# All packs from the fifth on turn their exponentials on VectorE and through DRAM; visits placed anew

## The chip, the cores and the metric

One core of one Trainium2 chip runs the whole program. The metric is the device time of that core in microseconds; a time given for a kernel is the median of its runs.

## The reference

Windowed attention of 8 heads (four with a plain window of 32, four with a window of 128 in steps of 4), followed by a gated feed-forward layer:

```python
def _attn_ref(q, k, v):                      # 8 x 8 x 576 x 64
    scores = scale * np.matmul(q, k.transpose(0, 1, 3, 2))
...
    masks = np.stack([mask_plain if h < H // 2 else mask_dil for h in range(H)], axis=0)
    scores = np.where(masks[None, :, :, :], scores, -1000000000.0)
    scores = scores - np.max(scores, axis=-1, keepdims=True)
    attn = np.exp(scores)
    attn = attn / (np.sum(attn, axis=-1, keepdims=True) + 1e-09)
    return np.matmul(attn, v)
...
def _moe_ref(x, w_gate, w_val, w_out):       # 4608 x 512, 512 x 1536, 1536 x 512
    g = x @ w_gate
    silu = g * (1.0 / (1.0 + np.exp(-g)))
    val = x @ w_val
    return (silu * val @ w_out)
```

## The kernel before, in words

**The feed-forward part** is most of the work. Every fp32 number is split into a high and a low part, and a product takes three matmuls (high by high, high by low, low by high). The 4608 tokens go in nine chunks of 512. The first three ("plain") chunks are computed as written: 39 `Item`s, each one block of 128 hidden columns (chunk 0 begins with six items of half width, 256 tokens). An item issues 12 matmuls for the gate into bank `bg` (`gv_mm(it, 0)`), 12 for the value into `bv` (`gv_mm(it, 1)`) and 12 into the four output banks `bo` (`out_mm`), the last ones an item late. Between them ScalarE takes the tanh of `bg` (`act_tanh`), VectorE multiplies twice (`dve_u`, `dve_h`), ScalarE writes the high part (`h_hi`) and GpSimd or VectorE the low part (`h_lo`). A product bank is written again two groups of 12 matmuls after it was filled. The other six chunks are computed by a Strassen scheme with products of 512 columns; it needs sums of weights, which VectorE and ScalarE prepare during the plain chunks (`mix_stage`) and the SyncE queue writes to the DRAM tensor `pieces`.

**The weights** come in 64-bit floating point. 24 units are loaded by SyncE (`w_load`, `at_int<-w`), turned into fp32 by ScalarE and VectorE, and split by ScalarE and by GpSimd (`at_float32r<-at_int`), all within chunk 0. Loading slots are few, so the load of a unit waits until VectorE is done with an earlier one.

**The attention part** comes in 38 packs of 128 x 504 scores, numbered `m` from 0: four packs for each of the first eight chunks, six for the last. Packs 0 to 3 give chunk 0, packs 4 to 7 chunk 1, packs 8 to 11 chunk 2. A pack is worked on in "visits", which the tables of numbers `EARLY`, `LATER` and `SLOTS` (L65 to L73) put at slots between the items: a slot is a third of an item (a group of 12 matmuls) up to slot 116, and one product after it. Chunk 1 begins at slot 45, chunk 2 at slot 81, the Strassen scheme at `SB` = 117. Visit `m` has three parts with a slot for each (`attend`, L886):

- part A: TensorE computes the attention output of an earlier pack `r` (`results`) and the scores of pack `m` (`scores`) into the PSUM tile `two`; VectorE masks, takes the maximum and subtracts it (`shift`), divides the output of pack `r` by its sums (`norm`) and turns it (`turn_y`); ScalarE takes the exponential (`exps`); SyncE loads the next pack's `qkb` and the pack's `vb`.
- part B: the exponentials of pack `m` are transposed, so that the next `results` can use them as weights.
- part C: the finished output of pack `r` is written into the chunk's input, high part by ScalarE, low part by GpSimd or VectorE (`x_copies`).

For part B there are two ways. Up to pack 11 (`m < TURNED`, L63) TensorE transposes four 128 x 128 blocks into PSUM (`turn_e`, L600) and ScalarE copies them to SBUF (`keys`, L604); then `r = m - 1`. From pack 12 on VectorE transposes blocks of 32 x 32 (`turn_far`, L617), SyncE stores the 256 KB to the DRAM tile `turned`, and four DMAs that ScalarE issues read it back in the order wanted (`load_far`, L625, in part A of visit `m + 1`); then `r = m - 2`, and visit `TURNED + 1` has no `results`.

From pack 4 on there is one SBUF buffer of each kind (L522): exponentials `e`, transposed `pt`, values `v`, output `y`. `turn_far` writes its transpose into the buffer `y`, which `norm`, `turn_y` and `x_copies` of pack `r` use too, so `norm` of the next visit waits until the store has read it.

**The order of the work** is written by `Desk`. The program text gives TensorE's order; each other engine's instructions are recorded with costs (L229) and put into an order of their own by a list scheduler (`issue`, L259), DMAs on SyncE and ScalarE among them. Every engine then runs its own list strictly in order. All these instructions appear with line L257 in the profile, those ahead of the recording with L238.

Of the kernel before, what the change touches and what calls it, by code (L numbers as in the profile page):

```python
# [25 lines left out]
NF = DFF // P  # L26
# [33 lines left out]
NSTART = 2  # L60
HALVED = 3
WARM = 9
TURNED = 12  # L63
FREE = 16000, 19500, 17500, 18000, 6000
EARLY = (-1, 1, None), (2, 3.5, 3), (5, 8, 6)  # L65
BEFORE = 3
# [2 lines left out]
ON_ACT = (2, 3, 4, 5, 6, 9, 11, 12, 15, 17, 19, 21, 23)  # L69
START = ("q0 q1 w v0 v1 w Q0 Q1 S0 X0 T0 W0 I3 I2 S1 K0 X1 W1 A0 W2 T1 J2 K1 W3 J2 N0 w U0 q2 v2 A1 q3 w w r W4 H0 W0 "  # L70
         "L0 N1 U1 H1 L1 W1 v3 W2 W3 W4")
LATER = (14, 3, 2), (23, 3, 4), (29, 7, 4), (39, 3, 2)
SLOTS = (1, 4, 7, 10, 13, 17, 20, 23, 27), (4, 13, 25, 37, 48, 58, 72, 84), (2, 11, 20, 29, 39, 47, 54, 65, 74, 84)  # L73
T0 = NPLAIN * CH
NB = S * 8 // CH - 1

# [258 lines left out]
def attention_moe(ctx, tc, qkb, vb, w, const, out):  # L335
# [276 lines left out]
    def at_n(m, n):  # L612

        g, j = divmod(n, NH)
        return n if m < TURNED else NG * j + g

# [205 lines left out]
    def idle(n, bank=k_bank[1]):  # L822
# [12 lines left out]
    first = {  # L835
        "Q": lambda m: scores(m, s_banks[m], True), "S": lambda m: shift(m, s_banks[m], fa, True),
        "X": exps, "T": lambda m: turn_e(m, k_bank[m]), "K": lambda m: keys(m, k_bank[m], fa),
        "A": lambda m: results(m, bank_r), "N": lambda m: norm(m, bank_r, fa),
        "U": turn_y, "H": lambda m: x_copy(m, "hi"), "L": lambda m: x_copy(m, "lo"),
        "q": lambda m: load_qk(m, fa, nc.sync, 2),  # L840
        "v": lambda m: load_v(m, fa, nc.sync, 2),
        "w": lambda m: w_load(3), "r": lambda m: ready.update(w=True), "I": lambda n: idle(n), "J": lambda n: idle(n, k_bank[0]), "W": lambda n: w_one(STAGES[n]),
    }
# [13 lines left out]
    SB = 3 * len(items)  # L857
# [3 lines left out]
    def visits(m, a, b, c):  # L861
        for what, n in zip("ABC", (a, b, c)):
            visit.setdefault(n, []).append((what, m))
# [2 lines left out]
        visits(2 + m, *x)  # L866
    for m, (a, b, c) in enumerate(LATER):
        visits(5 + m, a, a + b, a + c)
    for n in range(4):
        a = SB - 6 * NF + 3 + 25 * n // 3  # L870
        visits(9 + n, a, a + 4, a + 2)
    for n, a in enumerate(SLOTS[0]):
        visits(13 + n, SB - 3 * NF + a, SB - 3 * NF + a + 2, SB - 3 * NF + a + 1)
    first = 22
    for c in range(2):
        for a in SLOTS[1 + c]:
            a += SB + NSLOT * c
            visits(first, a, a + 6, a + 3)
            first += 1

    def ended(m):

        r = m - 1 if m <= TURNED else m - 2
        return r if r >= NSTART and m != TURNED + 1 else None

# [293 lines left out]
    for ci in range(NC):  # L1179
        base = SB + NSLOT * ci  # L1180
        first = n_out(ci, 0, 0)
# [18 lines left out]
        for t in range(NT):  # L1200
            for i in range(NP):
                n = n_out(ci, t, i)
# [59 lines left out]
```

## Time and profile before

| | |
|---|---|
| time, median of 3 runs | 906.27 us (906.18 to 907.73) |
| the profiled execution's own time | 907.4 us |
| its span, first to last instruction | 905.3 us |
| mean granted TensorE clock | 0.998 |
| TensorE matmuls busy | 893.0 us (99% of the span) |
| VectorE / ScalarE / GpSimd busy | 663.0 / 377.7 / 260.8 us (73 / 42 / 29%) |
| DMA | 218.44 MB, mean 241 GB/s |

The span is what the trace covers; the execution's own time is 2.1 us more. The profiled execution lies 1.1 us above the median of the runs.

### The profile page before, as it was taken

What the parts mean: (1) busy time and instruction counts of PE and PEld (TensorE: products, weight loads), DVE (VectorE), ACT (ScalarE), POOL (GpSimd) and SP (SyncE); (2) the same over time, 40 slices, a digit from 0 to 9 for tenths busy, and PEclk for the clock granted to TensorE, in tenths of its full rate; (3) what the DMA queues carried; (4) which work ended last, traced back from release to release, by engine and by line L of the source; (5) the groups of instructions that cost most, each with busy time, mean ns of one, the idle gap of its engine ahead of it and who ended that gap; (6) DMA issues with size and microseconds to landing.
All of it is one profiled execution on the core that took longest, in us unless ns stands there. A gap on an engine that the chain in (4) does not pass through costs nothing.

```text
span 905.3 us, 20915 instructions
## 1 busy us (share of the span) xinstructions
PE 893.0 (99%) x8610; PEld 732.9 (81%) x8610; DVE 663.0 (73%) x1001; ACT 377.7 (42%) x585; POOL 260.8 (29%) x177
## 2 busy tenths in 40 slices
PE   7899999999999999999999999999999999999998
PEld 5887888888878888888888888888888888888886
DVE  6888689888688564877779977878697746556752
ACT  5887433333233233333345543433355433334452
POOL 2569612221311111101132720111146401213451
PEclk9999999999999999999999999999999999999999
DMA  9999986444388751888787678889866675655562
GB/s 348 363 336 347 367 286 237 156 178 148 129 273 271 253 196 37 296 283 266 263 276 262 219 256 283 309 276 308 263 216 214 219 241 190 198 194 189 194 221 93
DMA packets 96142, 218.44 MB, mean 241 GB/s; under 512 B 9904, under 2 KB 37168, under 8 KB 96048
## 3 DMA queue, kind: packets, MB, share of 16 engines
q1 hardware_dynamic: 80928, 210.19, 67.9%
q10 hardware_dynamic: 15120, 6.92, 3.0%
q8 instruction: 68, 1.11, 0.5%
q14 instruction: 26, 0.21, 0.1%
HBM read 167.79 MB, written 49.28 MB: 240 GB/s over the span
## 4 chain that ended last, share of the span: by engine, by line
PE 89%; DMA 7%; DVE 1%; ACT 1%; issue 1%; POOL 0%; SPq 0%; ACTq 0%; DVEq 0%; POOLq 0%
PE bo L257 42%; PE bg L257 21%; PE bv L257 21%; PE two L257 5%; DMA at_int<-w 3%; DMA at_float<-turned 2%; DMA at_float<-qkb 1%; DVE at_int L257 1%; DMA at_float<-vb 1%; DVE at_float L257 0%; POOL at_float32r L257 0%; ACT at_int L257 0%; ACT at_float32r L257 0%; SPq L238 0%; ACTq L257 0%
## 5 line engine op out<-in xcount | busy, mean ns | idle before, releaser
L257 PE MATMUL bo<-at_float32r 128*128 128x512 f32 x1296 | 306.9, 391 | 0.0
L257 PEld LDWEIGHTS bo<-at_float32r 128*128 128x128 f32 x1296 | 242.4, 188 | 51.1
L257 POOL TENSOR_TENSOR at_float32r<-at_float,at_float32r 128x512 fp32r<-128x512 f32 (+1 forms) x109 | 161.2, 1483 | 376.1 <-ACT at_float32r L257 213.7
L257 ACT CAST at_float32r<-at_float 128x512 fp32r<-128x512 f32 (+2 forms) x214 | 147.7, 705 | 157.7 <-DVE at_float L257 76.9
L257 DVE TENSOR_TENSOR at_float<-bo,at_float 128x512 f32<-128x512 f32 x168 | 114.5, 686 | 99.7 <-ACT at_float L257 65.1
L257 DVE TENSOR_TENSOR at_float32r<-at_float,at_float32r 128x512 fp32r<-128x512 f32 (+1 forms) x105 | 114.2, 1103 | 49.2 <-ACT at_float32r L257 37.7
L257 PE MATMUL bg<-at_float32r 128*128 128x512 f32 x486 | 128.2, 390 | 0.0
L257 PE MATMUL bv<-at_float32r 128*128 128x512 f32 x486 | 128.0, 390 | 0.0
L257 ACT ACTIVATE at_float<-at_float 128x512 f32<-128x512 f32 (+1 forms) x108 | 68.0, 631 | 132.7 <-DVE at_float L257 112.1
L257 POOL TENSOR_TENSOR at_float<-at_float,at_float 128x512 f32<-128x512 f32 x36 | 51.0, 1416 | 223.4 <-DVE at_float L257 222.4
L257 PE MATMUL bg<-at_float32r,at_float32r 128*128 128x512 f32 (+1 forms) x468 | 108.6, 380 | 1.6 <-POOL at_float32r L238 0.9
L257 PEld LDWEIGHTS bv<-at_float32r 128*128 128x128 f32 x486 | 91.1, 188 | 19.0
L257 PEld LDWEIGHTS bg<-at_float32r 128*128 128x128 f32 x486 | 91.0, 188 | 19.1
L257 PE MATMUL bv<-at_float32r,at_float32r 128*128 128x512 f32 (+1 forms) x468 | 106.4, 377 | 0.0
L257 PE MATMUL bo<-at_float32r,at_float32r 128*128 128x512 f32 (+1 forms) x468 | 106.3, 376 | 0.0
L257 DVE SCALAR_TENSOR_TENSOR at_float<-at_float,at_float 128x512 f32<-128x512 f32 x144 | 104.8, 730 | 1.0
L257 PEld LDWEIGHTS bg<-at_float32r,at_float32r 128*128 128x128 f32 x468 | 83.4, 190 | 18.8 <-POOL at_float32r L238 1.3
L257 PEld LDWEIGHTS bv<-at_float32r,at_float32r 128*128 128x128 f32 x468 | 83.2, 189 | 16.4 <-DVE at_float L257 0.6
L257 PEld LDWEIGHTS bo<-at_float32r,at_float32r 128*128 128x128 f32 x468 | 82.9, 188 | 16.2
L257 ACT COPY at_float<-bg 128x512 f32<-128x512 f32 x63 | 36.9, 586 | 86.5 <-PE bg L257 78.2
L257 DVE TENSOR_TENSOR at_float<-at_float,at_float 128x512 f32<-128x512 f32 (+2 forms) x80 | 69.0, 873 | 1.6 <-POOL at_float L257 1.2
L257 ACT COPY at_float<-bv 128x512 f32<-128x512 f32 x63 | 37.0, 587 | 34.3 <-PE bv L257 29.7
(74 smaller groups left out, 610.8 us busy)
## 6 DMA issues: line engine op xcount, KB each, us to landing
at_float32r<-pieces SPq DMA_DIRECT2D x189, 512.0 KB, 4.0
pieces<-at_float32r SPq DMA_DIRECT2D x126, 256.0 KB, 4.4
at_float<-qkb SPq DMA_DIRECT2D x32, 576.0 KB, 7.3
at_float<-vb SPq DMA_DIRECT2D x34, 520.0 KB, 5.8
at_int<-w SPq DMA_DIRECT2D x38, 384.0 KB, 6.4
out<-at_float SPq DMA_DIRECT2D x36, 256.0 KB, 4.1
turned<-at_float SPq DMA_DIRECT2D x26, 256.0 KB, 4.0
at_float<-turned ACTq DMA_DIRECT2D x104, 64.0 KB, 6.8
```

The lines of the kernel that those rows point to most:

```text
L257: self.kept.append([engine, lambda: f(*a, **k), sorted(m for m in after if m >= 0), cost, later, both, start])
```

## The change

`TURNED` goes from 12 to 4: packs 4 to 11 take the way of `turn_far` and `load_far` as well. The visit without `results` is now visit 5 and no longer visit 13, and from visit 6 on a visit finishes pack `m - 2`. The slots are set anew so that each chunk's packs are finished where they were: chunk 0 gets five visits after the early ones (slots 14, 23, 28, 33, 39, part B three slots behind A and part C two) where it had four (14, 23, 29, 39); chunk 1 has four (49, 58, 66, 73) where it had four; chunk 2 has eight (83 to 108) where it had nine (82 to 108). The visits in the Strassen part keep their number and shift by up to two slots. The functions that are called are all there before.

```diff
--- before.py
+++ after.py
@@ -60,7 +60,7 @@
 NSTART = 2
 HALVED = 3
 WARM = 9
-TURNED = 12
+TURNED = 4
 FREE = 16000, 19500, 17500, 18000, 6000
 EARLY = (-1, 1, None), (2, 3.5, 3), (5, 8, 6)
 BEFORE = 3
@@ -69,8 +69,8 @@
 ON_ACT = (2, 3, 4, 5, 6, 9, 11, 12, 15, 17, 19, 21, 23)
 START = ("q0 q1 w v0 v1 w Q0 Q1 S0 X0 T0 W0 I3 I2 S1 K0 X1 W1 A0 W2 T1 J2 K1 W3 J2 N0 w U0 q2 v2 A1 q3 w w r W4 H0 W0 "
          "L0 N1 U1 H1 L1 W1 v3 W2 W3 W4")
-LATER = (14, 3, 2), (23, 3, 4), (29, 7, 4), (39, 3, 2)
-SLOTS = (1, 4, 7, 10, 13, 17, 20, 23, 27), (4, 13, 25, 37, 48, 58, 72, 84), (2, 11, 20, 29, 39, 47, 54, 65, 74, 84)
+LATER = (14, 3, 2), (23, 3, 2), (28, 3, 2), (33, 3, 2), (39, 3, 2)
+SLOTS = (4, 13, 21, 28), (2, 5, 8, 12, 16, 19, 23, 27), (2, 13, 23, 37, 48, 58, 72, 84), (4, 11, 19, 29, 37, 47, 54, 65, 74, 84)
 T0 = NPLAIN * CH
 NB = S * 8 // CH - 1
 
@@ -866,14 +866,14 @@
         visits(2 + m, *x)
     for m, (a, b, c) in enumerate(LATER):
         visits(5 + m, a, a + b, a + c)
-    for n in range(4):
-        a = SB - 6 * NF + 3 + 25 * n // 3
-        visits(9 + n, a, a + 4, a + 2)
-    for n, a in enumerate(SLOTS[0]):
-        visits(13 + n, SB - 3 * NF + a, SB - 3 * NF + a + 2, SB - 3 * NF + a + 1)
-    first = 22
+    first = 5 + len(LATER)
     for c in range(2):
-        for a in SLOTS[1 + c]:
+        for a in SLOTS[c]:
+            a += SB - 3 * NF * (2 - c)
+            visits(first, a, a + 4 - 2 * c, a + 2 - c)
+            first += 1
+    for c in range(2):
+        for a in SLOTS[2 + c]:
             a += SB + NSLOT * c
             visits(first, a, a + 6, a + 3)
             first += 1
```

How this moves instructions is shown at three places.

TensorE, chunk 0, the second half of the half-width items (`at_192_bfloat_61` is the identity, `at_512_float_124` the exponentials, `at_1024_float32r` the chunk's input), where part B of pack 4 stood; one piece of the difference:

```order
 L257 MATMUL bo_394<-at_512_float32r,at_1536_float32r 128x256
 L257 MATMUL bv<-at_1024_float32r,at_1536_float32r 128x256 x12
-L257 MATMUL two<-at_192_bfloat_61,at_512_float_124 128x128 x4
 L257 MATMUL bg<-at_1024_float32r,at_1536_float32r 128x256 x12
 L257 MATMUL bv<-at_1024_float32r,at_1536_float32r 128x256 x12
```

The four transposes are gone and nothing takes their place; the same holds for packs 5 to 11, eight times four instructions in all.

VectorE, part A of a visit in chunk 0 (`two` is the PSUM tile, `at_512_float_289` the buffer `y`, `at_512_float_124` the exponentials, `444` and `445` the two buffers of `dve_u` and `dve_h`). Before, visit 7 at slot 29:

```order
L257 TENSOR_TENSOR at_512_float_124<-two,at_384_bfloat_60 128x2x4x63
L257 TENSOR_SCALAR at_8_float_288<-two 128x8
L257 TENSOR_REDUCE at_8_float_238<-at_512_float_124 128x8
L257 RECIPROCAL at_8_float_288<-at_8_float_288 128x8
L257 TENSOR_TENSOR at_512_float_289<-two,at_8_float_288 128x8x2x32
L257 STREAM_TRANSPOSE at_512_float_289<-at_512_float_289 128x512
L257 SCALAR_TENSOR_TENSOR at_512_float_444<-at_512_float_444,bg 128x512
L257 TENSOR_TENSOR at_512_float_124<-at_512_float_124,at_8_float_238 128x2x4x63
```

Now, visit 8 at slot 33:

```order
L257 SCALAR_TENSOR_TENSOR at_512_float_444<-at_512_float_444,bv 128x512
L257 STREAM_TRANSPOSE at_512_float_289<-at_512_float_124 128x512
L257 SCALAR_TENSOR_TENSOR at_512_float_445<-at_512_float_445,bg 128x512
L257 TENSOR_SCALAR at_8_float_288<-two 128x8
L257 TENSOR_TENSOR at_512_float_124<-two,at_384_bfloat_60 128x2x4x63
L257 RECIPROCAL at_8_float_288<-at_8_float_288 128x8
L257 TENSOR_REDUCE at_8_float_227<-at_512_float_124 128x8
L257 TENSOR_TENSOR at_512_float_124<-at_512_float_124,at_8_float_227 128x2x4x63
L257 TENSOR_TENSOR at_512_float_289<-two,at_8_float_288 128x8x2x32
L257 SCALAR_TENSOR_TENSOR at_512_float_445<-at_512_float_445,bv 128x512
L257 STREAM_TRANSPOSE at_512_float_289<-at_512_float_289 128x512
```

The second row is `turn_far` of pack 7, which fills `y`; seven rows on, `norm` writes `y` again, and `dve_h` of the item stands behind it. Before, nothing but VectorE, ScalarE and GpSimd had to do with `y` here.

ScalarE, chunk 0, where the transposed exponentials of pack 6 come into the buffer `pt` (`at_512_float_241`; `turned_58` is a DRAM tile). Before:

```order
L257 ACTIVATE at_512_float_124<-at_512_float_124 128x8x63
L257 CAST at_512_float32r<-at_512_float_444 128x512
L257 CAST at_1536_float32r<-at_776_int_450 128x768
L257 CAST at_1536_float32r<-at_776_int_244 128x768
L257 COPY at_512_float_241<-two 128x512
L257 ACTIVATE at_1536_int_155<-at_1536_int_155 128x768
```

Now:

```order
L257 CAST at_512_float32r<-at_512_float_445 128x512
L257 ACTIVATE at_1536_int_155<-at_1536_int_155 128x768
L257 DMA at_512_float_241<-turned_58 32x4x128 x4
L257 ACTIVATE at_512_float_444<-bg 128x512
L257 CAST at_1024_float32r<-at_512_float_289 128x2x256
L257 ACTIVATE at_512_float_124<-at_512_float_124 128x8x63
L257 CAST at_1536_float32r<-at_1536_int_145 128x768
```

The copy from PSUM is gone. In its place four DMA issues stand directly ahead of an item's tanh (`at_512_float_444<-bg`), and they wait for the store of the same tile to land.

## Rows read from the trace of the kernel before

**Rows 1.** The page's part 1, busy time and instructions of each engine

```profile
PE 893.0 (99%) x8610; PEld 732.9 (81%) x8610; DVE 663.0 (73%) x1001; ACT 377.7 (42%) x585; POOL 260.8 (29%) x177
```

**Rows 2.** Waits of TensorE: who for whom, us in total, times, longest

```profile
PE two L257 <- DMA at_float<-qkb: 2.0, 3, 1.3
PE two L257 <- DMA at_float<-turned: 1.0, 2, 0.7
```

**Rows 3.** Timeline of TensorE, chunk 0: start, length, instructions [idle before]

```profile
107.56 2.88 PE L257 MATMUL bg<-at_float32r,at_float32r 128*128 128x512 f32 x12
110.29 0.60 PE L257 MATMUL two<-at_bfloat,at_float 128*128 128x128 f32 x4
110.64 3.00 PE L257 MATMUL bv<-at_float32r,at_float32r 128*128 128x512 f32 x12
113.48 2.89 PE L257 MATMUL bo<-at_float32r,at_float32r 128*128 128x512 f32 x12
```

**Rows 4.** Timeline of TensorE at the transposes of packs 4 and 5

```profile
40.46 0.74 PE L257 MATMUL bg<-at_float32r,at_float32r 128*128 128x256 f32 x4 [0.24 <-DVE at_float32r L257]
...
77.85 2.88 PE L257 MATMUL bo<-at_float32r,at_float32r 128*128 128x512 f32 x12
80.90 0.66 PE L257 MATMUL two<-at_bfloat,at_float 128*128 128x128 f32 x4 [0.17 <-ACT at_float L257]
```

**Rows 5.** Groups by shape: count, busy us, mean ns of one, idle before

```profile
L257 PE MATMUL two<-at_bfloat,at_float 128*128 128x128 f32 x36 | 5.5, 274 | 0.3 <-ACT at_float L257 0.2 <-DVE at_float L257 0.2
L257 ACT COPY at_float<-two 128x512 f32<-128x512 f32 x9 | 5.2, 580 | 1.6 <-PE two L257 1.6
L257 DVE STREAM_TRANSPOSE at_float<-at_float 128x512 f32<-128x512 f32 x62 | 43.8, 706 | 4.4 <-ACT at_float L257 3.4
L257 DVE TENSOR_TENSOR at_float<-two,at_float 128x512 f32<-128x512 f32 x36 | 24.7, 685 | 0.4
L257 DVE SCALAR_TENSOR_TENSOR at_float<-at_float,bv 128x512 f32<-128x512 f32 x33 | 22.6, 683 | 13.0 <-PE bv L257 12.5
```

**Rows 6.** The tile `turned`: issues (ns min/median/max), and landing times

```profile
L257 ACTq DMA_DIRECT2D at_float<-turned x104: 309/392/2067, 232.0 to 660.8; - x104
...
DMA to landing us min/median/max: 1.9/6.0/9.9
```

**Rows 7.** Three stretches of chunk 0: busy time by engine, clock, DMA share, GB/s

```profile
60.00:80.00 20.00, 19.97 (x215) 16.30 (x214) 19.24 (x21) 15.18 (x21) 16.19 (x9) 1.00 0.97 326
80.00:100.00 20.00, 19.83 (x211) 16.06 (x210) 17.81 (x20) 12.59 (x18) 17.30 (x10) 1.00 1.05 359
100.00:120.00 20.00, 20.00 (x180) 16.38 (x181) 12.81 (x22) 7.78 (x11) 8.12 (x5) 1.00 1.04 364
```

**Rows 8.** Timeline, GpSimd's weight splits and TensorE, chunk 0

```profile
50.65 4.18 POOL L257 TENSOR_TENSOR at_float32r<-at_int,at_float32r 128x768 fp32r<-128x768 f32 x2
...
62.23 2.91 PE L257 MATMUL bg<-at_float32r,at_float32r 128*128 128x512 f32 x12
...
70.82 0.80 PE L257 MATMUL two<-at_float,at_float 64*32 64x65 f32 x60
...
72.24 3.06 PE L257 MATMUL bg<-at_float32r,at_float32r 128*128 128x512 f32 x12
```

**Rows 9.** Timeline, ScalarE's queue and TensorE in chunk 2

```profile
257.06 1.98 ACTq L257 DMA_DIRECT2D at_float<-turned  x4
...
265.89 0.30 PE L257 MATMUL two<-at_float,at_float 64*32 64x65 f32 x2
266.93 0.78 PE L257 MATMUL two<-at_float,at_float 64*32 64x65 f32 x58 [0.74 <-DMA at_float<-turned]
```

**Rows 10.** DMA issues from 60 to 100 us: size, median us to landing

```profile
pieces<-at_float32r SPq DMA_DIRECT2D x23, 256.0 KB, 6.8
at_float<-qkb SPq DMA_DIRECT2D x2, 576.0 KB, 7.9
```

**Rows 11.** Waits of SyncE's queue: us in total, times, longest

```profile
SPq L257 <- DVE at_float32r L257: 74.7, 13, 11.0
```

## The prediction

> **What bounds the kernel now.** I began with the busy shares: TensorE has matmuls in flight for 893.0 of the 905.3 us [rows 1], so only a shorter list for TensorE, or a wait of TensorE that goes or comes, can move the time. Next I read TensorE's waits. The transfers of `qkb` and `turned`, the two that this change can touch, cost it 2.0 and 1.0 us in the whole span [rows 2]. In the three stretches of chunk 0 on which the change bears most, TensorE is busy for 19.97, 19.83 and 20.00 of 20 us [rows 7]. Then I went to the timeline to see what one set of transposes costs TensorE, and last to VectorE, the DMA engines and the queues, to see whether chunk 0 has room for what is added: VectorE is busy for 19.24, 17.81 and 12.81 of 20 us there, and the DMA share is 0.97 to 1.05 [rows 7]. So TensorE sets the pace, and close behind it in chunk 0 stand VectorE and the DMA.
>
> **What goes: 32 transposes on TensorE.** In the timeline I measure from start to start, since the ends of pipelined matmuls are modelled. A group of 12 starts at 107.56, and what follows it at 110.29: 2.73 us. The four transposes of a pack start there and the next group at 110.64: 0.35 us. That group takes 2.84 us to the start of the one after it, 113.48, which is 0.11 us over 2.73 [rows 3]. One pack costs 0.46 us. The mean of a single transpose, 274 ns [rows 5], would make 1.10 us of four; they overlap, and what counts is the distance of the starts.
> Eight packs lose theirs, but I count seven. Behind the transposes of pack 4, TensorE waits 0.24 us for VectorE's low part of the chunk's input [rows 4]; without the transposes it reaches that wait earlier and waits longer. Seven by 0.46 is **-3.22 us**; the eighth, another 0.46, is kept for the lower end.
> The transposes of pack 5 started at 80.90, although the group ahead of them, from 77.85, was through 2.73 us later, at 80.58 [rows 4]: 0.32 us in which they waited for ScalarE's exponential. VectorE's transpose takes over that wait, and TensorE has other work: **-0.32 us**.
>
> Here the Trainium skill speaks against the change: "VectorE: DVE Perf Modes", section "Rules for kernel authors", sends a 128 x 128 transpose to TensorE where PSUM will do as destination, as it does here. "TensorE: Matmul & The Clock Gate", section "Part 4: PE-mode transpose", puts one at about 275 ns in a kernel; the trace's 274 ns [rows 5] agrees. By that figure four would cost an estimated 1.10 us and seven packs 7.7 us, and the time would come out 4.5 us lower than mine, at 898.4. I stay with 0.46, the distance in the timeline [rows 3]; and a rule that prefers the engine with the shortest transpose is not one for a kernel in which that engine is the bound.
>
> **What is added beside it.** VectorE gets a transpose of 706 ns per pack, ScalarE loses a copy of 580 ns [rows 5] and gets four DMA issues, 1.98 us together in one far visit [rows 9]. SyncE gets a store of 256 KB per pack, the four loads read as much. Eight transposes are 5.6 us of VectorE, of which five packs, 3.5 us, fall into chunk 0. There is also one more visit between 70 and 120 us than before, with some 4 us for its masking, maximum, division and turn, while the visit at slot 14 gets lighter by as much. Against these 3.5 and 4 us VectorE has 0.8, 2.2 and 7.2 us free in the three stretches [rows 7]. It fits if weight work can slip to the third stretch. Can it? The two units that the item at 62.23 us begins with were split at 54.83, 7.4 us ahead [rows 8], in the stretch where VectorE is fullest; so a slip of a few us is covered. If that cover were gone, each us of slip would be one of TensorE.
> The DMA engines get 0.5 MB a pack, 2.6 MB for five packs in chunk 0, 7 us at 359 GB/s [rows 7]. They are full until 120 us, but with writes of `pieces` among the rest, which nobody reads until the Strassen part. What is late next is thus `pieces`, at no cost.
>
> **Waits that go and come.** In chunk 2 the far way is there already. A visit's first matmul went at 265.89, and the rest only at 266.93, since the four loads issued from 257.06 on had not landed: 0.74 us [rows 9]. Both waits for `turned`, 1.0 us in all [rows 2], are at visits three slots behind another. Chunk 2 has six such distances before and three now, so I take half of it: **-0.5 us** (ends: -1.0 and 0).
> In chunk 0 the distances are longer. From the visit at 70.82 us [rows 8] to the next, at slot 28, lie 1.42 us of its own and five groups: 15 us. A far pack needs inside a visit's distance 0.8 us until the buffer `pt` is free, 2.0 us of issues and 6.0 us to land, 9.9 at most [rows 6, 9]: 9 to 13 us. A `qkb` of the next pack lands 7.9 us after its issue in that stretch [rows 10], and it is issued behind a visit and several `pieces`. The room is 2 to 6 us, if the store of the tile does not come late. For the three visits at slots 28, 33 and 39 the lower end is 0, and the upper end 3.3 us, once the longest wait for a `qkb`, 1.3, at two of them and at the third the longest for `turned`, 0.7 [rows 2]. I take **+0.7 us**, one wait of the size seen, because the rows nearest to it, those of chunk 2 with its shorter distances, show only two such waits in nine visits.
> The Strassen part's visits move by two slots at most and keep seven or more between them, as before: 0.
>
> **Sum.** -3.22 - 0.32 - 0.5 + 0.7 = -3.34 us. The profiled execution's 907.4 us becomes 904.06; the median of the runs lies 1.13 us lower, so I predict **902.9 us** against 906.27. About 0.2%, 1.8 us, is what a measurement can tell from no change.
>
> **Rivals.**
> *A store stands behind another DMA on SyncE's list (slower).* There is one buffer `y`. VectorE's division of the next visit waits until the store of the transposed tile has read it, and in VectorE's list `dve_h` stands right behind. A product bank is written again two groups, 5.46 us, after it is full; with 0.69 us for the division and 0.68 for `dve_h` [rows 5] the store may be 4.1 us late before TensorE stops. SyncE has been held by one DMA that waited for VectorE's low parts for up to 11.0 us [rows 11]; a turned store behind such a one costs 11.0 - 4.1 = 6.9 us, and the time is 902.2 (my sum without new waits) + 6.9 = 909.1. For it: in chunk 0 the queue is full of such DMAs, and four stores go through it after slot 23. Against it: the list is ordered with the store's time in it, and chunk 2 runs the same way with one slot between part B and the next A. Chance 0.08.
> *The loads come late in chunk 0 (no change).* With the DMA share at 1.0 the store lands like the `pieces` there, 6.8 us [rows 10], the loads at 9.9 [rows 6] instead of 6.0, and visits 7 to 9 wait for 3 us more in all than I took: 905.9. Against it: the 2 to 6 us of room. "DMA: Bandwidth & Descriptors" of the Trainium skill, section "Issuing engines are not separate DMA queues", says that ScalarE's DMAs run on the same 16 engines and interleave with SyncE's, so they would share the full engines; no row here shows such loads at a share of 1.0. Chance 0.10.
> *Weights set the pace of chunk 0 (no change).* Then TensorE waits for what the transposes of packs 4 to 8 leave, as at 40.46 us [rows 4], and only packs 9 to 11 count: 3 x 0.46 + 0.5 less, 0.7 more, 905.1. Against it are the 7.4 us of lead [rows 8] and 0.03 to 0.17 us of idle time in 20 [rows 7]. Chance 0.04.
> That the transposes stay is excluded: TensorE's list has 32 fewer.
>
> **The numbers.** My forecast, a gain of over 1.8 us, has 0.78. No change takes the second and third rival, 0.14; slower the first, 0.08. The range: the lower end is all eight packs (-3.68), the 0.32, the whole 1.0 and no new wait, 901.3, taken as 901.2; the upper one 902.2 with new waits of 3.3 us, 905.5. It holds the third rival and leaves out the first, most of the second, and some chance of more gain below.
>
> **What would show it.** The group of transposes into `two` falls from 36 to 4, TensorE's busy time falls by 3 to 5 us (32 x 5.5/36 at most [rows 5]), VectorE's transposes rise from 62 to 70. TensorE's waits on `qkb` and `turned` together should stay under 4 us, and the weights' lead over 3 us. It is wrong if a single wait of over 2 us stands in TensorE's list before 140 us, or if groups of 12 start more than 2.8 us apart in chunk 0 while VectorE's division waits for a store.

## The result, and the profile after

The changed kernel takes 916.96 us (median of five runs, 911.87 to 919.39) against 906.40 us beside it: 1.0099 times the time, with a 95% interval of 1.0075 to 1.0123. I had predicted 902.9 us. The profiled execution took 919.39 us, the longest of the five; its span is 917.3 us, 12.0 more than before.

The page's part 1 and the instruction queue of its part 3 (packets, MB, share):

```profile
PE 895.3 (98%) x8578; PEld 732.7 (80%) x8578; DVE 655.1 (71%) x1009; ACT 371.2 (40%) x577; POOL 260.2 (28%) x177
...
q8 instruction: 68, 1.11, 0.5%
```

Groups by shape, which answer to [rows 5]:

```profile
L257 DVE STREAM_TRANSPOSE at_float<-at_float 128x512 f32<-128x512 f32 x70 | 49.3, 705 | 10.5 <-ACT at_float L257 7.4 <-POOL at_float32r L257 2.0
...
L257 PE MATMUL two<-at_bfloat,at_float 128*128 128x128 f32 x4 | 0.6, 279 | 0.0
```

TensorE's 36 transposes are 4, VectorE's 62 are 70, and TensorE has 32 matmuls fewer than in [rows 1], yet it is busy for 2.3 us more. Its waits, which answer to [rows 2], say where to look:

```profile
PE two L257 <- issue: 6.2, 4, 3.1
PE two L257 <- DMA at_float<-turned: 3.0, 2, 2.1
PE bg L257 <- DVE at_float L257: 2.9, 2, 2.0
PE two L257 <- DMA at_float<-qkb: 1.4, 3, 0.6
```

"Issue" is a wait for nothing that the profile shows. Two of the four are long. The timeline of TensorE around the first, in chunk 2:

```profile
270.82 0.80 PE L257 MATMUL two<-at_float,at_float 64*32 64x65 f32 x60
...
271.48 0.76 PE L257 MATMUL two<-at_float 64*32 64x63 f32 x55
274.57 0.31 PE L257 MATMUL two<-at_float 64*32 64x63 f32 x7 [2.33 <-issue]
274.81 4.58 PE L257 MATMUL bg<-at_float32r,at_float32r 128*128 128x512 f32 x12
279.23 2.88 PE L257 MATMUL bv<-at_float32r,at_float32r 128*128 128x512 f32 x12
...
315.50 0.34 PE L257 MATMUL two<-at_float 64*32 64x63 f32 x15 [3.12 <-issue]
315.78 4.59 PE L257 MATMUL bo<-at_float32r,at_float32r 128*128 128x512 f32 x12
```

TensorE stops inside the scores of a visit, between two matmuls whose data are there alike. Queue q8 brings TensorE's own program, 68 packets of 16 KB: the trace has 17,409 instructions of TensorE (weight loads, matmuls and semaphore instructions), 68 times 256. The queue carried nothing from 263.6 to 272.1 us; then, in 272.1:273.2, by the view of the DMA queues:

```profile
q8 instruction: 1, 0.02, 5.4%
```

and TensorE went on 1.5 us after the end of that packet. At 315.50 it was the same, with nothing from 303.3 to 313.2 and one packet in 313.2:314.3. So it looks as if the engine had run out of instructions; the experiments test it.

The group of 12 behind each stop takes 4.4 us to the next start (274.81 to 279.23), not 2.73 [rows 3]: 1.7 us lost. The clock says why, in the windows by stage (PEclk is the third number from the end):

```profile
60.00:80.00 20.00, 18.80 (x202) 14.75 (x201) 14.57 (x20) 12.06 (x17) 13.69 (x7) 1.00 0.99 329
80.00:100.00 20.00, 17.95 (x200) 14.44 (x199) 18.26 (x21) 14.06 (x19) 15.92 (x10) 1.00 1.00 326
100.00:120.00 20.00, 20.00 (x203) 16.09 (x203) 10.69 (x18) 7.21 (x11) 9.04 (x7) 0.91 1.02 346
260.00:280.00 20.00, 17.66 (x313) 14.17 (x312) 14.52 (x28) 4.79 (x8) 2.81 (x2) 0.91 0.81 258
300.00:320.00 20.00, 15.97 (x305) 12.94 (x305) 11.54 (x22) 4.76 (x7) 1.31 (x1) 0.91 0.90 281
```

A granted clock of 0.91 is a stretch at 1.2 GHz among 2.4. TensorE is "busy" through it, which is how its busy time rises with fewer matmuls. The third such stretch follows a wait in chunk 0:

```profile
94.84 2.88 PE L257 MATMUL bo<-at_float32r,at_float32r 128*128 128x512 f32 x12
99.77 4.61 PE L257 MATMUL bg<-at_float32r,at_float32r 128*128 128x512 f32 x12 [2.05 <-DVE at_float L257]
104.31 0.81 PE L257 MATMUL two<-at_float,at_float 64*32 64x65 f32 x60
...
573.26 0.78 PE L257 MATMUL two<-at_float,at_float 64*32 64x65 f32 x58 [2.06 <-DMA at_float<-turned]
```

VectorE's first product of an item came late there (its timeline stands under "Chunk 0" below). In 60:80 and 80:100 TensorE lost 1.2 us and 2.1 us, where [rows 7] has next to nothing. The last row is a wait in the Strassen part.

**The sum.** Waits on issue in the scores 5.45, half clock 1.7 + 1.7 + 1.8, VectorE and GpSimd in chunk 0 3.3 (2.05 at 99.77, 0.89 at 79.43, 0.32 at 75.71), `turned` 2.0 more, `qkb` 0.6 less: +15.35 us. The span grew by 12.0, so 3.35 us were won, about what the transposes were priced at. By the whole idle time of TensorE, 9.7 us more than before, in place of the waits picked out here, it is 2.9.

To see where each version wins and loses, I take the start of the same product matmul in each kernel (all have the same 3672 in the same order; the columns are seven of them, by their start in the kernel before) less its start before, in us:

| | 14.9 | 94.0 | 110.6 | 253.3 | 333.2 | 605.6 | 901.0 |
|---|---|---|---|---|---|---|---|
| the change | -0.38 | -1.84 | +3.40 | +2.21 | +9.27 | +12.32 | +12.02 |
| e2 | +3.90 | +3.30 | +3.31 | +3.27 | +14.06 | +14.05 | +14.50 |
| e9 | +6.01 | +4.72 | +4.72 | +4.68 | +4.95 | +4.86 | +4.70 |
| e10 | +0.40 | +0.01 | +0.01 | -1.71 | -1.62 | -1.62 | -1.68 |
| e11 | +0.57 | -2.08 | -0.78 | -1.18 | -1.61 | -1.70 | -0.11 |
| e14 | +1.76 | -0.73 | +0.89 | -1.43 | -1.79 | -1.90 | -2.05 |
| e17 | +0.03 | -2.57 | -1.30 | -1.40 | +7.96 | +9.18 | +8.87 |
| e16 | +0.54 | -2.23 | -0.96 | -3.27 | -3.85 | -3.96 | -4.11 |

Each row is one profiled execution. From 94.0 to 110.6 every version with five visits in chunk 0 pays 1.3 us or more, its additional visit, and has it back in chunk 2.

### The profile page after: what moved, and what is told of

It reads as the page before. It is cut to its first block, busy times and chain, and to the rows that moved or that the text cites. A ratio compares the mean times of both kernels' runs of the same rounds, so it can differ in the third digit from the quotient of the medians.

```text
span 917.3 us, 20921 instructions
## 1 busy us (share of the span) xinstructions
PE 895.3 (98%) x8578; PEld 732.7 (80%) x8578; DVE 655.1 (71%) x1009; ACT 371.2 (40%) x577; POOL 260.2 (28%) x177
## 4 chain that ended last, share of the span: by engine, by line
PE 89%; DVE 4%; DMA 3%; issue 1%; ACT 1%; ACTq 1%; POOL 0%; SPq 0%; DVEq 0%
PE bo L257 41%; PE bg L257 22%; PE bv L257 21%; PE two L257 5%; DMA at_float<-turned 2%; DVE at_int L257 1%; DVE at_float L257 1%; DVE at_float32r L257 1%; DMA at_int<-w 1%; ACTq L257 1%; ACT at_float32r L257 0%; POOL at_float32r L257 0%; ACT at_int L257 0%; DMA pieces<-at_float32r 0%; SPq L238 0%
## 5 line engine op out<-in xcount | busy, mean ns | idle before, releaser
L257 PE MATMUL bg<-at_float32r,at_float32r 128*128 128x512 f32 (+1 forms) x468 | 111.5, 387 | 4.6 <-DVE at_float L257 2.9
L257 PEld LDWEIGHTS bg<-at_float32r,at_float32r 128*128 128x128 f32 x468 | 85.6, 195 | 23.5 <-DVE at_float L257 3.8
L257 DVE TENSOR_TENSOR at_float<-at_float,at_float 128x512 f32<-128x512 f32 (+2 forms) x80 | 65.9, 834 | 1.6 <-POOL at_float L257 1.2
L257 DVE STREAM_TRANSPOSE at_float<-at_float 128x512 f32<-128x512 f32 x70 | 49.3, 705 | 10.5 <-ACT at_float L257 7.4
```

The costliest lines, as they stand in the source:

```text
L257: self.kept.append([engine, lambda: f(*a, **k), sorted(m for m in after if m >= 0), cost, later, both, start])
```

## The experiments

### Where the visits lie in the program (e1, e2, e9)

A visit is 128 small matmuls with 128 weight loads, 256 instructions in 1.4 us; 16 KB of program are 256 instructions as well. Counted from the first instruction, each weight load, each pass of a matmul and each semaphore instruction as one, the two stops stand 24.76 and 28.76 blocks of 256 into the program. The theory: a visit that begins shortly behind such a point outruns the fetch of the next block. The test shifts everything by instructions that do nothing else.

```diff
     idle(WARM)
+    for _ in range(22):      # 32 in e1, 64 in e9
+        nc.tensor.matmul(out=k_bank[1][:32, :8], lhsT=ones[:, :32], rhs=ones[:, :8], start=True, stop=True)
```

e1, the changed kernel with 32. Expected:

> The changed kernel with 32 tiny fp32 matmuls (32 x 8, never read) put behind the warm-up ones, 128 more instructions for TensorE, while it waits for the first loads; all later work lies half a block of 256 instructions further on in TensorE's program. Theory A (the two waits marked issue, 2.33 us at 274.57 and 3.12 us at 315.50, and the half-clock stretch behind each come from where a visit of 256 instructions lies against the blocks of 256 in which the program is fetched): both are gone or shrink below 1 us in all, and the clock is 1.0 in 260:280 and 300:320; 5.45 + 2 x 1.7 = 8.9 us less than the changed kernel's 917 us, so about 908 us (906 to 911). Theory B (the fetch is late because the store and the four loads of the exponentials fill the DMA engines): the waits stay between 250 and 330 us, 915 to 919 us. Under both the stalls of chunk 0 stay.

Measured: 916.45 us, 1.013 (1.0093 to 1.0167). Both stops are gone and the clock is 1.00 in 260:280 and 300:320; but stops of 1.81 and 1.59 us stand at 36.57 and 636.20, 5.76 and 56.76 blocks into the program, and the 32 matmuls cost 2 us at the start, which I had not reckoned. The place moved as theory A says; the time did not fall, and theory A's 906 to 911 us were missed. (The time is in theory B's range, but the two waits that B would have kept are gone.)

e2, the kernel before with 22. Expected:

> The kernel before with 22 of the same tiny matmuls, 88 instructions: two visits of chunk 2 (the fifth from the last and the second from the last ahead of the Strassen part, roughly 270 and 310 us) now begin 0.86 and 0.83 of a block into the program, as the two that stalled in the changed kernel began at 0.81 and 0.87. Nothing of the change is in it. Theory A (position against the fetched blocks): one or two waits marked issue of 2 to 3 us inside the scores, each with a stretch at half clock behind it, 4 to 9 us in all, so 910 to 915 us. Theory B (transfers of the exponentials): these are as in the kernel before, so 906 to 907 us.

Measured: 916.32 us, 1.0109 (1.0060 to 1.0159), a little over theory A's 910 to 915, with nothing of the change in it. TensorE's timeline at the two visits that were named beforehand:

```profile
289.54 0.71 PE L257 MATMUL two<-at_float 64*32 64x63 f32 x49
292.06 0.34 PE L257 MATMUL two<-at_float 64*32 64x63 f32 x13 [1.81 <-issue]
...
326.42 0.75 PE L257 MATMUL two<-at_float 64*32 64x63 f32 x51
331.91 0.44 PE L257 MATMUL two<-at_float 64*32 64x63 f32 x10 [4.74 <-issue]
332.28 5.43 PE L257 MATMUL bg<-at_float32r,at_float32r 128*128 128x512 f32 x12
```

They stand at 26.76 and 30.76 blocks. By the table, 3.9 us go at the start and 10.8 us between 253.3 and 333.2, in the slowest of its four runs (911.93 to 921.89).

e9, the control: 64 tiny matmuls, a whole block. Expected:

> The kernel before with 64 of the tiny matmuls, 256 instructions, a whole block: every visit stands again where it stood in its block. It is the control for the 22 that cost 10 us. Theory A (position in the block): 906 to 907.5 us, no wait marked issue over 1 us after 60 us. Rival (the tiny matmuls cost in themselves, by a later or colder start): 912 us or more, more than with 22.

Measured: 913.57 us, 1.0061 (1.0042 to 1.0079), outside both forecasts; both had a part of it. In the profiled execution everything lost is lost at the start, and from there on the table's row is flat; no wait on issue over 1 us stands behind 60 us. TensorE's timeline shows the start:

```profile
0.98 8.73 PE L238 MATMUL fx<-at_float 128*64 128x512 f32 x134 [0.98 <-DVE at_float L238]
9.65 0.60 PE L238 MATMUL fs<-at_bfloat 128*128 128x252 bf16 x2
```

With the block whole, all visits stand where they stood and the stops are gone: what cost 10.8 us in e2 was the place. The page of e9 counts one packet more on q8 than the 68 before, for 256 instructions more:

```profile
q8 instruction: 69, 1.13, 0.5%
```

### Half visits (e5 to e8)

Scores one slot behind the attention output (two in the Strassen part), to give the fetch time:

```diff
         for what, n in zip("ABC", (a, b, c)):
             visit.setdefault(n, []).append((what, m))
+        if m >= SPLIT and m < NPK:
+            visit.setdefault(a + (1 if a < SB else 2), []).append(("S", m))
```

> The changed kernel with every visit from the 14th on in two halves: attention outputs (128 instructions of TensorE) at the slot, scores (the other 128) one slot later in chunk 2, two slots later in the Strassen part. Nothing else is changed. The shifted kernels showed the waits marked issue always at the same place in the blocks of 256 instructions (0.76 of a block as counted here), inside visits, and in the kernel before as well once it was shifted. Theory A: a visit takes a whole block in 1.4 us, faster than the next block can be fetched if it was asked for just before; two half bursts with a group of 12 between them (2.7 us) give the fetch that time. The waits marked issue in `two` then fall from 5.45 us to under 1 us, with them two half-clock stretches: 907 to 911 us. Rival: half a block in 0.7 us outruns the fetch as well, or the fetch is late by more than 2.7 us: stalls of 1 to 3 us stay, now at the start of either half: 912 to 917 us.

> The kernel before with the 22 tiny matmuls that made it 10 us slower (its waits of 2.0 and 4.7 us marked issue at 290 and 327 us), and now its visits from the 14th on in the same two halves. Theory A: both waits go, 906 to 908 us, as the kernel before without the 22. Rival (fetch too late for half bursts as well): 910 to 916 us. The halves themselves cost nothing that I know of: if waits on turned grow because the scores come a slot later, 1 us more.

Measured: 921.10 us (1.0154) and 921.75 us (1.0154). The waits on issue in the scores are gone in both, e2's 6.5 us too, as theory A says; yet both are slower. The timeline of e6:

```profile
374.16 0.86 PE L258 MATMUL two<-at_float,at_float 64*32 64x65 f32 x64
374.95 3.01 PE L258 MATMUL bo<-at_float32r 128*128 128x512 f32 x12
377.89 0.85 PE L258 MATMUL two<-at_float 64*32 64x63 f32 x64
378.68 1.66 PE L258 MATMUL bo<-at_float32r 128*128 128x512 f32 x6
```

A half is 0.79 us from start to start and the group of 12 behind it 2.94, not 2.73 [rows 3]: 1.0 us twice, against 1.42 + 0.2 for a whole visit [rows 4, 8]. 24 visits by 0.4 are some 9 us, a cost that I had expected to be nothing. e7 and e8, which add other cures to it, pay it too:

> The kernel with the new way from pack 8 on (four visits in chunk 0, 911.0 us with waits marked issue of 3.3 us), with the Strassen slots of before and visits in two halves. If the three causes are all there are, what is left is the gain of four packs: 906.4 - 4 x 0.46 - 0.5 = 904 us (903 to 905.5), without a wait of over 1 us for issue, turned or VectorE after 60 us. Rival (a cause not yet named): 907 us or more.

> The changed kernel (new way from pack 4 on) with the Strassen slots of before, visits in two halves, and the five visits of chunk 0 seven slots apart (11, 18, 25, 32, 39) in place of 14, 23, 28, 33, 39. Theory D1 (the three visits five and six slots apart crowd VectorE between 65 and 100 us): TensorE's waits on VectorE and GpSimd in chunk 0 fall from 3.3 to under 1 us and the clock stays 1.0 from 100 us on: 902 to 904.5 us. Theory D2 (chunk 0 has no room for a fifth visit and the far way, wherever they lie): waits of 2 to 5 us there, 906 to 911 us.

Measured: 914.80 (1.0095) and 921.92 us (1.0149). The forecast of 904 us for e7 was missed, as were both for e8, 911 at most. Five visits seven slots apart still leave waits on VectorE before `bg` of 5.2 us in e8, 2.5 of them in chunk 0 and 2.7 at 147.75, in chunk 1: another spacing of the visits did not cure it.

### The Strassen part (e3)

```diff
-... (2, 13, 23, 37, 48, 58, 72, 84), (4, 11, 19, 29, 37, 47, 54, 65, 74, 84)
+... (4, 13, 25, 37, 48, 58, 72, 84), (2, 11, 20, 29, 39, 47, 54, 65, 74, 84)
```

> The changed kernel with the visits of the Strassen part at the slots of before (from 7 to 9 slots between its eighth and tenth visit, and all others as they were). Theory C (the wait of 2.06 us for turned at 573.26 comes from the seven slots to the visit before): that wait goes, 2 us less, 915 us (913 to 916.5), TensorE's waits on turned below 1.5 us. Rival: the transfers are late for another reason, or the wait turns up at a neighbour: 916.5 to 918 us. The two waits marked issue at 274 and 315 us stay, since the program up to there is the same.

Measured: 913.55 us, 1.0071 (1.0048 to 1.0094), against 1.0099. The intervals overlap, but in the profile the wait is gone, and `turned` costs 0.7 us in all:

```profile
PE two L257 <- DMA at_float<-turned: 0.7, 1, 0.7
```

The stops on issue stand at 24.76 and 28.76 blocks as in the changed kernel. This fits theory C. But e17, with the slots of the changed kernel, has 0.93 us at this visit (570.15), and e1 none for `turned`, so the seven slots do not bring the wait in every run.

### Chunk 0 (e4, e12, e14, e15, e17)

e4 takes the new way only from pack 8 on:

```diff
-TURNED = 4
+TURNED = 8
-LATER = (14, 3, 2), (23, 3, 2), (28, 3, 2), (33, 3, 2), (39, 3, 2)
+LATER = (14, 3, 2), (23, 3, 4), (29, 7, 4), (39, 3, 2), (44, 3, 2)
```

> The changed kernel with the new way only from pack 8 on: chunk 0 has its four visits of before (slots 14, 23, 29, 39, packs 4 to 7 transposed by TensorE), and the visit without results is the ninth, at slot 44. Four packs then save 0.46 us each. Theory D (the fifth visit and the far way in chunk 0 make ScalarE and VectorE late, 3.3 us of TensorE's waits at 75 to 100 us, and the half clock from 100 us on, 1.7 us): both go. Theory A says that the waits at 274 and 315 us go as well, because chunk 2 lies 28 instructions further on in the program and no visit begins at 0.80 to 0.88 of a block behind one at 0.5 to 0.6: 906.4 - 1.8 - 0.5 + 2.1 (the wait at 573, which stays) = 906 us (904.5 to 907.5). Against A but with D: 917 - 5 + 1.8 = 914 us. Against both: 917 us.

Measured: 911.04 us, 1.0045 (1.0024 to 1.0066); 904.25 to 915.12 in ten runs. Chunk 0 is without loss, as D says. Stops on issue of 3.3 us in all stand at 24.76 and 31.76 blocks: theory A had forecast none at either place, so my rule for which visits stall was wrong, and the spread suggests that the stops do not come in every run.

With that known, two versions at the old slots of chunk 2 and of the Strassen part, shifted so that from chunk 2 on every instruction lies in its block as in the kernel before (e10: pack 8 on, 7 tiny matmuls; e11: pack 4 on, 14):

```diff
+SLOTS = (4, 13, 21, 28), (4, 7, 10, 13, 17, 20, 23, 27), (4, 13, 25, 37, 48, 58, 72, 84), (2, 11, 20, 29, 39, 47, 54, 65, 74, 84)
```

> The new way from pack 8 on, chunk 0 with its four visits of before, the eight visits of chunk 2 and all of the Strassen part at the slots that these packs had before (4, 7, 10, 13, 17, 20, 23, 27 in chunk 2), and 7 tiny matmuls so that from chunk 2 on every instruction of TensorE stands where it stood in its block in the kernel before, but for one instruction (255 of 256). If A, C and D are all there is: 906.4 - 4 x 0.46 - up to 0.5 = 904.3 us (903.3 to 905.5), without a wait marked issue over 1 us behind 60 us. Rival (the fetch is late at random, wherever the visits lie, and the kernel before has it less for another reason): 907 to 912 us, as the same way without this placing took 911.0.

> The changed kernel (new way from pack 4 on, five visits in chunk 0) with the same slots in chunk 2 and the Strassen part as that one, and 14 tiny matmuls for the same places in the blocks. What is left against it is chunk 0 alone: its waits on VectorE and GpSimd (3.3 us) and the half clock behind (1.7 us), against four packs' transposes (1.8 us): 907.5 us (905.5 to 910), and the waits for turned under 1.5 us in all. Rival (chunk 0 costs nothing by itself, the 3.3 us are lead lost that would be lost elsewhere): 903 to 904.5 us. If the places don't matter: 912 us or more.

Measured: e10 905.30 us, 0.9975 (0.9964 to 0.9985); e11 908.84 us, 1.0014 (1.0000 to 1.0027). Both lie in their ranges, though e11's waits for `turned` come to 1.6 us, 1.15 of them at 627.94, and not under 1.5. Only packs 4 to 7, worked on in chunk 0, are left against e11. Is it the fifth visit or the new way? e12 is e10 with five visits in chunk 0:

```diff
-LATER = (14, 3, 2), (23, 3, 4), (29, 7, 4), (39, 3, 2), (44, 3, 2)
+LATER = (14, 3, 2), (23, 3, 2), (28, 3, 2), (33, 3, 2), (39, 3, 2)
```

> The version that took 905.3 us (new way from pack 8 on, all work from chunk 2 on at its old places in the blocks, 7 tiny matmuls), but with chunk 0's five visits at 14, 23, 28, 33, 39 as in the changed kernel: visits 5 to 8 finish packs 4 to 7 with TensorE's transposes, and the one without results, whose scores are those of pack 8, comes at slot 39 in place of 44. Theory D1 (the fifth visit's masking, maximum and division, crowded into 65 to 100 us, make VectorE and ScalarE late): 2 to 5 us are lost in chunk 0 as in the changed kernel, 907.5 to 910 us, with waits on VectorE or GpSimd of over 1.5 us in all between 65 and 110 us. Theory D2 (the new way: VectorE's transposes, stores and loads between those five visits): nothing is lost there, 904.5 to 906 us.

Measured: 904.81 us, 0.9975 (0.9960 to 0.9989). The new way, then, and not the fifth visit. ScalarE's timeline in the changed kernel shows how it could hold chunk 0 up (ACTq are its DMA issues):

```profile
50.20 0.38 ACT L257 ACTIVATE at_float<-bg 128x256 f32<-128x256 f32 x1 [0.26 <-PE bg L257]
50.28 2.49 ACTq L257 DMA_DIRECT2D at_float<-turned  x3
54.07 0.41 ACT L257 CAST at_float32r<-at_float 128x256 fp32r<-128x256 f32 x1 [3.49 <-DMA at_float<-turned]
54.10 0.31 ACTq L257 DMA_DIRECT2D at_float<-turned  x1
...
65.16 0.89 ACT L257 ACTIVATE at_int<-at_int 128x768 f32<-128x768 f32 x1 [4.29 <-DMA at_int<-w]
...
67.46 0.58 ACT L257 ACTIVATE at_float<-bg 128x512 f32<-128x512 f32 x1
```

For 3.5 us ScalarE computes nothing while it issues loads and waits. Later a unit's weights came 4.29 us late (65.16), and a tanh (67.46) stands behind them. GpSimd's last split of weights, in the kernel before and in the changed one:

```profile
106.55 1.87 POOL L257 TENSOR_TENSOR at_float32r<-at_int,at_float32r 128x768 fp32r<-128x768 f32 x1 [3.19 <-ACT at_float32r L257]
```

```profile
116.66 1.88 POOL L257 TENSOR_TENSOR at_float32r<-at_int,at_float32r 128x768 fp32r<-128x768 f32 x1 [1.82 <-ACT at_float32r L257]
```

Ten us later. The six runs in which ScalarE issues the loads of packs 4 to 8 (the changed kernel, e1, e3, e5, e8, e11) have this split between 114.74 and 120.09; the kernel before, e4, e10 and e12 to e17 have it between 104.33 and 106.66. TensorE did not wait for that unit, though. Its 2.05 us at 99.77 were a wait for VectorE, which did three weight steps ahead of the item's product:

```profile
93.65 5.47 DVE L257 SCALAR_TENSOR_TENSOR at_int<-at_int 128x768 int32<-128x768 int32 x3
99.05 0.67 DVE L257 SCALAR_TENSOR_TENSOR at_float<-at_float,bg 128x512 f32<-128x512 f32 x1
```

In e11 VectorE's order is the same up to 130 us and ScalarE pauses as long, but the three steps took half the time, and TensorE has no wait over 0.73 us between 60 and 112 us in that execution (906.94 us, the fastest of twelve):

```profile
55.05 0.41 ACT L257 CAST at_float32r<-at_float 128x256 fp32r<-128x256 f32 x1 [3.49 <-DMA at_float<-turned]
91.30 2.69 DVE L257 SCALAR_TENSOR_TENSOR at_int<-at_int 128x768 int32<-128x768 int32 x3
```

And e1 has a wait of 2.05 us at 102.04 without such a pause of ScalarE. So the pause alone does not decide; what does is open. e14 takes the issues from ScalarE in e11, e15 adds the bytes alone to e12:

```diff
-            nc.scalar.dma_start(out=t[BQ * b ...
+            (nc.sync if m < 9 else nc.scalar).dma_start(out=t[BQ * b ...
```

```diff
                     keys(m, turned_at, pool_of(m))
+                    if m >= 2 * NSTART:
+                        for x in spare:
+                            nc.sync.dma_start(out=x, in_=st[m]["pt"])
```

> The changed kernel with the old places in chunk 2 and the Strassen part (the run that took 908.8 us, 1.0014 of the kernel before), but the four loads of packs 4 to 8 are issued by SyncE in place of ScalarE. Theory E1 (ScalarE's list is held by the issues and by their wait for the store): ScalarE's wait of 3.5 us for turned at 50 us goes, and so do 2 us or more: 905 to 906.8 us, 0.9985 to 1.000 of the kernel before. Theory E2 (the bytes make weights late, whoever issues): 908 to 910 us; SyncE's list, where weights stand behind these loads, may make it worse, 910 us or more.

> The run with five visits and TensorE's transposes in chunk 0 (904.8 us, 0.9975 of the kernel before), and behind the copy of each transposed tile of packs 4 to 7 two stores of 256 KB each to DRAM that nobody reads: the bytes of a pack's store and loads (2.1 MB in all), issued by SyncE, without VectorE's transposes and without ScalarE's issues and waits. Theory E2 (bytes): ScalarE's waits for at_int<-w in 36:112 rise from 6.1 to 8 us or more, and 2 to 4 us are lost in chunk 0: 907 to 909 us. Theory E1 (ScalarE's issues): 904.5 to 906 us.

Measured: e14 904.98 us, 0.9974 (0.9963 to 0.9984), 3.9 us less than e11. e15 905.87 us, 0.9982 (0.9973 to 0.9991), and ScalarE's waits for `at_int<-w` are 3.1 us: the bytes cost about 1 us, with intervals that overlap. So E1's time came, and E2's did not: issuing by SyncE was worth 3.9 us. The mechanism inside is not shown. The same line lets the scheduler put the lists in a new order: from the first of these loads on, SyncE's list differs, and VectorE's three weight steps no longer stand together. Nor does e11's profile lose the time up to 110.6 us: by the table it is behind e14 only from 253.3 on, after a wait of 1.08 us for GpSimd at 140.55, and loses 1.15 us more at 627.94. "DMA: Bandwidth & Descriptors" of the Trainium skill, section "Issuing engines are not separate DMA queues", says that issuing from several engines at once saves only the sequencer's time, usually small beside the DMA; here the choice of the engine for five packs' 20 issues was worth 3.9 us, with the new order of the lists in it.

e17 is the changed kernel with this one line:

> The changed kernel as it is, but for the loads of packs 4 to 8, issued by SyncE: one cure alone. It should take the 4 us that it took from the run with the old places, and leave the waits marked issue in chunk 2 and the wait for turned near 573 us: 917 - 4 = 913 us (911 to 915), 1.005 to 1.009 of the kernel before. If chunk 0 was more than that: 910 us. If chunk 0's share was already the half clock of later stalls: 916 us.

Measured: 909.42 us, 1.0028 (1.0008 to 1.0047), 905.22 to 915.93: more than the 4 us forecast, and nearest to "chunk 0 was more than that". The last split is back at 104.68:

```profile
104.68 1.87 POOL L257 TENSOR_TENSOR at_float32r<-at_int,at_float32r 128x768 fp32r<-128x768 f32 x1 [1.82 <-ACT at_float32r L257]
```

By the table its profiled execution is 1.30 us ahead at 110.6 where the change is 3.40 behind, and then loses 9.4 us in chunk 2 to two stops on issue (24.76 and 28.76 blocks) and the slow groups behind them; it is the slowest of its twelve runs.

### All cures (e13, e16)

The tiny matmuls had cost the start. The same shift comes from cutting the three warm-up matmuls into ten (e13, else e10) or 17 (e16, else e14; the edit shown is e16's):

```diff
-    idle(WARM)
+    idle(1)
+    for _ in range(2 * WARM - 2):
+        nc.tensor.matmul(out=k_bank[1][:D, :D], lhsT=ones, rhs=ones, start=True, stop=True)
```

> The version that took 905.3 us without its 7 tiny matmuls: the 28 instructions come from cutting the three warm-up matmuls into ten with the same columns in all, so that nothing is added to the start but the overhead of smaller matmuls. The tiny ones had set the first product 0.4 us back. Expected: 904.9 us (904 to 906), by 0.2% faster than the kernel before or a little more, with no wait marked issue over 1 us behind 60 us. If the start is not what they cost: 905.3 us.

> The new way from pack 4 on, as in the changed kernel, with the three cures: loads of packs 4 to 8 issued by SyncE, visits of chunk 2 and the Strassen part at the slots their packs had before, and the same places in the blocks from chunk 2 on (254 of 256), got by cutting the three warm-up matmuls into 17 with the same columns and not by tiny ones, which cost about 1 us of start in the run of 905.0. Expected: 904 us (903 to 905), 0.9955 to 0.997 of the kernel before. Rival: ten smaller warm-up matmuls more cost the start as much as the tiny ones: 905 us.

Measured: e13 903.97 us, 0.9968 (0.9956 to 0.9979); e16 **903.14 us, 0.9950 (0.9933 to 0.9967)**. Page and waits of e16:

```profile
PE 887.9 (99%) x8606; PEld 731.1 (81%) x8606; DVE 655.1 (73%) x1009; ACT 371.3 (41%) x577; POOL 257.4 (29%) x177
```

```profile
PE bg L257 <- POOL at_float32r L238: 1.3, 2, 0.7
PE bg L257 <- DVE at_float L257: 1.2, 2, 1.0
PE fk L238 <- issue: 1.1, 1, 1.1
PE bv L257 <- issue: 1.0, 1, 1.0
```

No wait of TensorE is over 1.1 us, and its busy time is 5.1 us below [rows 1]; 1.7 of them are clock, since the granted clock was 0.83 in 15:25 in the profiled execution of the kernel before and 1.00 in this one. All eight packs take the new way here: with nothing paid elsewhere, the change is worth about the 4 us that it set out to win.

## Why the prediction was wrong, point by point

- **The transposes, -3.22 and -0.32: right.** 3.35 us were won in the changed kernel by the sum above, and e16 is 4.1 us ahead at the end. Its 903.14 us lie beside my 902.9, but for a kernel that is not the change.
- **"What is added beside it": the step that failed in chunk 0.** I counted ScalarE's four issues as 1.98 us [rows 9] that lie beside other work, and let "a slip of a few us" be covered by 7.4 us of lead [rows 8]. I did not ask what stands behind the issues in ScalarE's list. It is the weights and an item's tanh; the weights ended ten us later, more than the lead, and TensorE waited 3.3 us in chunk 0 for products and low parts that VectorE and GpSimd made late. That is part of the third rival, "weights set the pace of chunk 0", at which I put 0.04 and 905.1. That the way of issuing brought it, e14 and e17 show, at 3.9 and 7.5 us between medians; by which wait it did so stays open.
- **A term that the sum lacked: the fetch of TensorE's program.** It is the largest: 5.45 us of stops and 3.4 us of half clock behind them. The kernel before has no such stop behind 60 us, and none of the views that I read showed the risk; e2 shows that 88 instructions bring it out there. Removing transposes and moving visits re-laid every later visit against the blocks.
- **"The Strassen part's visits: 0": wrong.** Seven slots between visits existed before, but elsewhere in the scheme; here the round trip of `turned` came 2.06 us late. e3 went from 1.0099 to 1.0071, with intervals that overlap.
- **New waits in chunk 0, +0.7: the wait was elsewhere.** The visits there did not wait for `qkb` or `turned`. The turned waits of chunk 2 did not halve either: 0.92 us stood at 311.06 alone.
- **A wait of 2 us was priced at 2 us.** With the slow group behind it, the 2.05 us in chunk 0 cost 3.9 and the 2.33 us in chunk 2 cost 4.0. Not every such wait costs that: see the last section.
- **The first rival (a store behind another DMA): not seen.** In the changed kernel the division waited for no store; in e3 and e11 it did once, 0.95 and 1.20 us, without a wait of TensorE behind it.
- **What would show it.** The two limits I set were both passed: a wait of 2.05 us before 140 us, and `qkb` with `turned` at 4.4 us. The counts of transposes came as said; TensorE's busy time rose by 2.3 us where I had it fall by 3 to 5.

What stays open: what decides when the next block is asked for. e4 stalled at two places that I held safe, and e1 in the Strassen part; the runs show that the place matters and at which point of a block TensorE runs dry (0.76, as counted here), not which places are safe. Nor is it known how issuing by ScalarE made chunk 0 late.

## What to carry to other kernels

Where the bounding engine executes bursts of very short instructions, shift its program by some harmless ones before you credit or blame a change of instruction count: this change cost 1%, and gained 0.5% once its places, its issuing queue and its slots were set otherwise. A DMA issue is an instruction in its engine's list: ask what stands behind it there, and try another queue. And price a wait of some 2 us of TensorE with the slower clock that can follow it.

## What the runs showed of the hardware that I had not expected

- TensorE's program arrives during execution in packets of 16 KB, 256 instructions each (68 packets, 69 with 256 instructions more). A visit uses up one in 1.4 us, and the stops counted here behind 60 us took 0.8 to 4.7 us. Taking each packet for the block that begins at the next place 0.76, the packets of the changed kernel start 0.01 to 1.17 blocks ahead of their use, and the two at 0.01 are those of the two stops. "Runtime: NRT & Kernel Launch" of the Trainium skill, section "Instruction fetch mechanics", gives the same block and calls the cost of crossing a boundary "mostly hidden"; for these bursts the measurement decides otherwise.
- Behind waits of 2.05, 2.33 and 3.12 us the granted clock was 0.91 in the mean over 20 us, and the next group of 12 took 4.4 to 4.5 us; behind 4.74 us it took 5.27 (332.28 to 337.55). Behind the 2.06 us at 573.26 the group kept its 2.9 us, and behind 2.05 us at 102.04 in e1 and 2.11 us at 273.63 in e3 the granted clock stayed at 1.00. So a wait of this size can bring the lower clock, and need not.
- Tiny matmuls are not free where TensorE seems to be waiting for its first data: 64 of them set the first product back by 6.0 us, and the two bf16 matmuls behind them took 0.60 us, against 0.38 in the kernel before.
